# Folding the later batches' sums of squares to a pair of bf16 rows on the VectorE, in a chunk that the scores have left

## The chip, the cores and the metric

The kernel runs on one core of a Trainium2 chip. The metric is the device time of one execution in microseconds (us), over several executions. The profile is one execution with every instruction recorded; its span is 1.9 to 2.0 us shorter than the time. PE is the TensorE (matmuls), PEld its weight loads, DVE the VectorE, ACT the ScalarE, POOL the GpSimd.

## The reference

Attention over channels ("cross-covariance"), then a gated feed-forward layer on all tokens. There are 4 batches of 6016 tokens with 256 channels. Cut to what matters here:

```python
qn = q / (np.linalg.norm(q, axis=1, keepdims=True) + 1e-06)   # norm over the 6016 tokens
kn = k / (np.linalg.norm(k, axis=1, keepdims=True) + 1e-06)
s = kn.transpose(0, 2, 1) @ qn / tau                          # 256 x 256 per batch
a = softmax(s)                                                # per row
x = (v @ a).reshape(B * S, D)
out = (sigmoid(x @ w_gate) * (x @ w_val)) @ w_out
```

## The kernel before

A batch's tokens lie as 47 row tiles of 128 tokens, in 12 chunks (row groups) of up to four tiles; the last has three. While PE runs the feed-forward of batch b, it also works on the scores and norms of batch n = b + 1, spread over "slots". A chunk has 12 slots (FC = 12), and a slot is one gate/value pair with four output matmuls of the chunk before:

```python
for ci in range(NCH):                      # 12 chunks
    block = b + 1 < B and ci in (9, 10)    # these do their output matmuls at the end
    for f in range(FC):                    # 12 slots
        glu(b, ci, f)                      # 4 matmuls of 512 columns, sigmoid on ACT, hT multiply on DVE
        flush()                            # output copies that have become ready, on DVE
        if prev is not None and not block:
            out_mms(*prev, f * TPC, (f + 1) * TPC)   # 4 matmuls of 256 columns
        for fn, a in side.get((ci, f), ()):          # scores, squares, norms of batch n
            fn(*a)
    ...
```

`ps_gate` and `ps_val`, the PSUM buffers that a slot's matmuls write, have two copies each. The value matmul of slot f + 2 must wait until the hT multiply of slot f has read its buffer.

The side work of the next batch: a score is two matmuls of 256 columns per row tile. DVE squares q and k of each group and adds the squares into bf16 accumulators of four rows. The norm step sums these over the partitions with matmuls against ones:

```python
first, last = (14 if b == 0 else 0), 9 * FC
for g, (t0, nt) in enumerate(groups):
    s0 = first + g * (last - first) // NCH
    at(max(0, s0 - 20), load_qk, n, t0, nt)
    for u in range(nt):
        at(first + (t0 + u) * (last - first) // NT, score, n, t0, u)
    ...
    for i, (fn, w) in enumerate(((acc_square, 0), (acc_add, 0), (acc_square, 1), (acc_add, 1))):
        at(s0 + 1 + 2 * i, fn, n, g, w)
at(9 * FC + 9, norms_mm, n)

def norms_mm(b):
    ...
    norm_mms(ps, (acc_q,), TPC, True, True, (0,))     # 4 rows x 2 halves, one column each
    for u in range(TPC):                              # 4 rows, 256 columns each
        mm(ps[:, CB:], ones_bf, acc_k[:, u, :], False, u == TPC - 1, skip_group_check=True)
```

Of the kernel before, what the change touches and what calls it, by code (L numbers as in the profile page):

```python
# [9 lines left out]
FP32 = mybir.dt.float32  # L10
BF16 = mybir.dt.bfloat16
ACT = mybir.ActivationFunctionType
ALU = mybir.AluOpType
# [4 lines left out]
def kernel(  # L18
# [20 lines left out]
    nc = tc.nc  # L39
    P = nc.NUM_PARTITIONS  # L40
# [4 lines left out]
    B, N, C = q.shape  # L45
# [3 lines left out]
    CB = C // P  # L49
    FC = DFF // P  # L50
    FG = 512
    NFG = DFF // FG
    TPC = 4
# [12 lines left out]
    def pool(name, bufs, **kw):  # L66
        return ctx.enter_context(tc.tile_pool(name=name, bufs=bufs, **kw))
# [4 lines left out]
    attp = pool("attp", 1)  # L72
# [14 lines left out]
    def mm(out, lhsT, rhs, start, stop, **kw):  # L87
        nc.tensor.matmul(out, lhsT=lhsT, rhs=rhs, start=start, stop=stop, **kw)  # L88
# [33 lines left out]
    ones_bf = consts.tile([P, P], BF16)  # L122
# [14 lines left out]
    for fg in range(NFG):  # L137
        for w, src in enumerate((moe_w_gate, moe_w_val)):
            nc.gpsimd.dma_start(
                out=w_sb[w][fg],  # L140
                in_=src.rearrange("(t p) f -> p t f", p=P)[:, :, ds(fg * FG, FG)],
# [5 lines left out]
    st = {}  # L147
# [33 lines left out]
    def norm_mms(ps, sqs, nt, first, last, order=(0, 1)):  # L181

        for w in order:
            sq = sqs[w]
            for u in range(nt):
                for j in range(CB):
                    mm(
                        ps[:, w * CB + j : w * CB + j + 1],
                        sq[:, u, ds(j * P, P)],
                        ones_bf[:, 0:1],  # L190
                        start=(first and w == order[0] and u == 0 and j == 0),
                        stop=(last and u == nt - 1),
                        skip_group_check=True,
                    )
# [15 lines left out]
    def acc_add(b, g, w):  # L210
# [5 lines left out]
            out=acc[:, :nt, :], in0=acc[:, :nt, :], in1=st[b]["sq", w][:, :nt, :], op=ALU.add  # L216
        )

    def norms_mm(b):

        s = st[b]
        acc_q, acc_k = s["acc"]
        ps = psm.tile([P, CB + C], FP32, tag="m", name="ps_n")
        norm_mms(ps, (acc_q,), TPC, True, True, (0,))
        for u in range(TPC):
            mm(ps[:, CB:], ones_bf, acc_k[:, u, :], False, u == TPC - 1, skip_group_check=True)
        s["n"] = ps

    def wide_sqrt(b):
# [136 lines left out]
    def transpose_v(b, ci, ps=None, late=None):  # L366

        t0, nt = groups[ci]
        v_sb = vs.pop((b, ci))
        vT = vtpool.tile([P, TPC * CB, P], BF16, tag="vT", name="vT")  # L370
        flat = v_sb[:, :nt, :].rearrange("p t c -> p (t c)")
        if ps is None:
            nc.sync.dma_start_transpose(out=vT[:, : nt * CB, :], in_=flat)
        else:
            for n in range(nt * CB):
                nc.tensor.transpose(  # L376
                    out=ps[:, n, :], in_=flat[:, ds(n * P, P)], identity=ident_bf
                )
            half = nt * CB // 2
            nc.vector.tensor_copy(out=vT[:, :half, :], in_=ps[:, :half, :])  # L380
            (nc.scalar.copy if late is None else late)(vT[:, half : nt * CB, :], ps[:, half : nt * CB, :])
        vts[b, ci] = vT.rearrange("p (u cb) n -> p cb u n", cb=CB)
# [65 lines left out]
    acc = st[0]["acc"]  # L448
# [50 lines left out]
    def side_work(b):  # L499


        side = {}

        def at(slot, fn, *a):
            side.setdefault(divmod(slot, FC), []).append((fn, a))

        for ci in range(NCH):
            nb, nci = (b, ci + 1) if ci + 1 < NCH else (b + 1, 0)
            lb, lci = (b, ci + 2) if ci + 2 < NCH else (b + 1, ci + 2 - NCH)
            if (nb, nci) == (0, 1):  # L510
                at(7, lambda: transpose_v(0, 1, psm.tile([P, TPC * CB, P], BF16, tag="m", name="ps_tp")))
            elif nb < B:
                at(ci * FC + 2, transpose_v, nb, nci)
            if lb < B:
                at(ci * FC + 0, load_v, lb, lci)
        n = b + 1
        if n == B:
            return side
        first, last = (14 if b == 0 else 0), 9 * FC
        for g, (t0, nt) in enumerate(groups):  # L520
            s0 = first + g * (last - first) // NCH
            at(max(0, s0 - 20), load_qk, n, t0, nt)
            for u in range(nt):
                at(first + (t0 + u) * (last - first) // NT, score, n, t0, u)
            if g == 0:
                at(s0, acc_start, n)
            for i, (fn, w) in enumerate(((acc_square, 0), (acc_add, 0), (acc_square, 1), (acc_add, 1))):
                at(s0 + 1 + 2 * i, fn, n, g, w)
        at(9 * FC + 9, norms_mm, n)
        for ci, s, *call in (  # L530
            (9, 0, wide_sqrt, n),
            (9, 2, wide_inv, n, 0),
            (9, 3, wide_inv, n, 1),
            (10, 0, wide_scale, n),
            (10, 0, exps, n, 0),
            (10, 0, exps, n, 1),
        ):
            side.setdefault((ci, FC + s), []).append((call[0], call[1:]))
        at(11 * FC + 0, sums_both, n)
        at(11 * FC + 0, gh_tiles, n)  # L540
        for i in range(len(gh_order)):
            at(11 * FC + min(i + 1, FC - 1), gh, n, i, *((pss, "s"), (psm, "m"))[i % 2])
        return side
# [3 lines left out]
    for b in range(B):  # L547
        side = side_work(b)
        for ci in range(NCH):
            block = b + 1 < B and ci in (9, 10)  # L550
            for f in range(FC):
                glu(b, ci, f)
                flush()
                if prev is not None and not block:
                    out_mms(*prev, f * TPC, (f + 1) * TPC)
                for fn, a in side.get((ci, f), ()):
                    fn(*a)
                if (b, ci) == (0, 0) and f < len(gh_order) - 5:
                    gh(0, 5 + f, pso, "o")
            if prev is not None and block:  # L560
                for s in range(TPC):
                    for fn, a in side.get((ci, FC + s), ()):
                        fn(*a)
                    out_mms(*prev, s * FC, (s + 1) * FC)
                    flush()
            prev = (b, ci)
# [38 lines left out]
```

## Time and profile before

| | before |
|---|---|
| time, median of 6 runs | 831.43 us (831.34 to 831.52) |
| span of the profiled run | 829.6 us |
| PE busy | 817.8 us (99%), 5224 matmuls |
| DVE busy | 581.1 us (70%), 998 instructions |
| norm matmuls of the later batches | 24 of one column, 12 of 256 columns |

PE is the bound. Its matmuls overlap in the record, so the cost of one is read from the start of one to the start of the next. The prediction shows the lines.

### The profile page before, as it was taken

What the parts mean: (1) busy time and instruction counts of PE and PEld (TensorE: products, weight loads), DVE (VectorE), ACT (ScalarE), POOL (GpSimd) and SP (SyncE); (2) the same over time, 40 slices, a digit from 0 to 9 for tenths busy, and PEclk for the clock granted to TensorE, in tenths of its full rate; (3) what the DMA queues carried; (4) which work ended last, traced back from release to release, by engine and by line L of the source; (5) the groups of instructions that cost most, each with busy time, mean ns of one, the idle gap of its engine ahead of it and who ended that gap; (6) DMA issues with size and microseconds to landing.
All of it is one profiled execution on the core that took longest, in us unless ns stands there. A gap on an engine that the chain in (4) does not pass through costs nothing.

```text
span 829.6 us, 13793 instructions
## 1 busy us (share of the span) xinstructions
PE 817.8 (99%) x5224; PEld 503.6 (61%) x5224; DVE 581.1 (70%) x998; ACT 391.9 (47%) x644; POOL 83.3 (10%) x159
## 2 busy tenths in 40 slices
PE   7899999999999999999999999999999999999998
PEld 4556666666666666665576666666566566666666
DVE  6577777777667777777767777777766666666664
ACT  4654444445644444444654444444655444444442
POOL 5531100002110100000210020000000000000000
PEclk9999999999999999999999999999999999999999
DMA  9999724326755553233874453233222323322211
GB/s 209 207 206 185 134 52 90 51 62 131 135 107 102 102 108 62 51 52 84 156 140 100 84 113 73 51 78 63 61 61 64 71 51 83 70 49 69 46 36 71
DMA packets 78739, 77.19 MB, mean 93 GB/s; under 512 B 50768, under 2 KB 55632, under 8 KB 78672
## 3 DMA queue, kind: packets, MB, share of 16 engines
q0 software_dynamic: 23920, 38.81, 28.3%
q1 hardware_dynamic: 54608, 36.97, 17.4%
q8 instruction: 41, 0.67, 0.3%
q10 hardware_dynamic: 144, 0.52, 0.2%
q14 instruction: 26, 0.21, 0.1%
HBM read 78.64 MB, written 24.64 MB: 125 GB/s over the span
## 4 chain that ended last, share of the span: by engine, by line
PE 95%; DMA 3%; POOL 0%; issue 0%; ACT 0%; DVE 0%; POOLq 0%; ACTq 0%
PE ps_o L88 30%; PE ps_val L88 29%; PE ps_gate L88 29%; PE ps_s L88 4%; DMA k_sb<-in_k_dram 3%; PE ps_gh L88 3%; PE ps_n L88 0%; PE ps_busy L88 0%; POOL q_sb L97 0%; ACT e_sb L294 0%; DVE hT L406 0%; ACT g_sb L405 0%; POOL k_sb L97 0%; PE ps_rk L88 0%; PE ps_tp L376 0%
## 5 line engine op out<-in xcount | busy, mean ns | idle before, releaser
L406 DVE TENSOR_TENSOR hT<-ps_val,g_sb 128x512 bf16<-128x512 f32 (+1 forms) x576 | 391.5, 680 | 214.6 <-ACT g_sb L405 209.3
L405 ACT ACTIVATE g_sb<-ps_gate 128x512 bf16<-128x512 f32 (+1 forms) x576 | 338.5, 589 | 386.0 <-PE ps_gate L88 378.4
L88 PE MATMUL ps_gate<-vT,gh_G 128*128 128x512 bf16 (+1 forms) x1152 | 337.7, 375 | 0.4 <-ACT g_sb L405 0.4
L88 PE MATMUL ps_val<-vT,gh_H 128*128 128x512 bf16 (+1 forms) x1152 | 337.5, 375 | 0.1
L88 PE MATMUL ps_o<-w_out_sb,hT 128*128 128x256 bf16 x2256 | 326.2, 273 | 0.0
L88 PEld LDWEIGHTS <-hT 128*128 128x128 bf16 x2256 | 220.8, 98 | 124.7
L88 PEld LDWEIGHTS <-gh_H 128*128 128x128 bf16 x1152 | 112.7, 98 | 131.0 <-issue 0.4
L88 PEld LDWEIGHTS <-gh_G 128*128 128x128 bf16 x1152 | 112.4, 98 | 38.0 <-issue 0.6
L106 POOL DMA_DIRECT2D v_sb<-in_v_dram x48 | 25.6, 534 | 623.6 <-DMA vT<-v_sb 501.3
L432 DVE COPY out_sb<-ps_o 128x256 f32<-128x256 f32 x188 | 77.9, 414 | 13.5 <-PE ps_o L88 13.5
L88 PE MATMUL ps_s<-k_sb,q_sb 128*128 128x256 bf16 x376 | 66.0, 272 | 5.6 <-DMA k_sb<-in_k_dram 4.3
L88 PEld LDWEIGHTS <-q_sb 128*128 128x128 bf16 x376 | 36.6, 98 | 14.7 <-issue 6.8
L215 DVE TENSOR_TENSOR acc<-acc,sq 128x1024 bf16<-128x1024 bf16 (+1 forms) x66 | 44.2, 670 | 0.0
L176 DVE TENSOR_TENSOR sq<-q_sb 128x1024 bf16<-128x1024 bf16 (+2 forms) x44 | 29.4, 668 | 2.7 <-DMA q_sb<-in_q_dram 2.7
L97 POOL DMA_DIRECT2D q_sb<-in_q_dram x48 | 26.4, 550 | 15.3 <-DMA q_sb<-in_q_dram 6.2
L97 POOL DMA_DIRECT2D k_sb<-in_k_dram x48 | 26.2, 545 | 13.9 <-DMA k_sb<-in_k_dram 8.6
L176 DVE TENSOR_TENSOR sq<-k_sb 128x1024 bf16<-128x1024 bf16 (+2 forms) x34 | 22.4, 658 | 0.9 <-ACT sq L174 0.9
L359 ACT ACTIVATE gh_G<-ps_gh,rrow 128x512 bf16<-128x512 f32 x21 | 14.4, 688 | 12.7 <-PE ps_gh L88 10.9
L88 PE MATMUL ps_busy<-ones_wide,ones_bf 128*128 128x512 bf16 x60 | 17.0, 416 | 1.6 <-DVE shift L127 1.6
L174 ACT ACTIVATE sq<-k_sb 128x1024 bf16<-128x1024 bf16 (+1 forms) x11 | 11.2, 1019 | 14.6 <-DMA k_sb<-in_k_dram 14.6
L361 DVE TENSOR_SCALAR gh_H<-ps_gh,rrow 128x512 bf16<-128x512 f32 x22 | 16.4, 744 | 1.6 <-PE ps_gh L88 1.6
L455 DVE TENSOR_TENSOR acc<-acc,sq 128x1024 bf16<-128x1024 bf16 x16 | 11.1, 692 | 5.6 <-ACT sq L174 5.4
(59 smaller groups left out, 117.7 us busy)
## 6 DMA issues: line engine op xcount, KB each, us to landing
out_dram<-out_sb SPq DMA_DIRECT2D x44, 512.0 KB, 2.9
v_sb<-in_v_dram POOLq DMA_DIRECT2D x44, 256.0 KB, 3.9
q_sb<-in_q_dram POOLq DMA_DIRECT2D x43, 256.0 KB, 7.0
k_sb<-in_k_dram POOLq DMA_DIRECT2D x43, 256.0 KB, 7.7
out_dram<-out_sb SPq DMA_DIRECT2D x4, 384.0 KB, 2.5
w_gate<-in_moe_w_gate_dram POOLq DMA_DIRECT2D x3, 256.0 KB, 6.8
w_val<-in_moe_w_val_dram POOLq DMA_DIRECT2D x3, 256.0 KB, 7.4
w_out_sb<-in_moe_w_out_dram POOLq DMA_DIRECT2D x1, 768.0 KB, 12.6
```

Source lines behind the costliest of these rows:

```text
L88: nc.tensor.matmul(out, lhsT=lhsT, rhs=rhs, start=start, stop=stop, **kw)
L97: nc.gpsimd.dma_start(out=tl[:, :nt, :], in_=rows(src, b)[:, t0 : t0 + nt, :])
L106: nc.gpsimd.dma_start(out=v_sb[:, :nt, :], in_=rows(v, b)[:, t0 : t0 + nt, :])
L174: nc.scalar.activation(out=sq[:, :nt, :], in_=src[:, :nt, :], func=ACT.Square)
L176: engine.tensor_tensor(out=sq[:, :nt, :], in0=src[:, :nt, :], in1=src[:, :nt, :], op=ALU.mult)
L215: nc.vector.tensor_tensor(out=acc[:, :nt, :], in0=acc[:, :nt, :], in1=st[b]["sq", w][:, :nt, :], op=ALU.add)
L359: nc.scalar.activation(out=dst, in_=ps, func=ACT.Copy, scale=r)
L361: nc.vector.tensor_scalar(out=dst, in0=ps, scalar1=r, scalar2=None, op0=ALU.mult)
L405: nc.scalar.activation(out=g_sb[:, :n], in_=ps_gate[:, :n], func=ACT.Sigmoid)
L406: nc.vector.tensor_tensor(out=hts[b, ci][:, f, :n], in0=ps_val[:, :n], in1=g_sb[:, :n], op=ALU.mult)
L432: nc.vector.tensor_copy(out=out_sb[:, s, :], in_=ps)
L455: nc.vector.tensor_tensor(out=acc[w], in0=acc[w], in1=sq[w], op=ALU.add)
```

## The change

The intent is to take matmuls off the engine that sets the time. DVE folds the four accumulated rows to one fp32 row, and stores it as two bf16 numbers: the rounded value and what the rounding lost. The norm step then reads two rows in place of four. To make room on DVE, the scores, squares and adds are spread over eight chunks in place of nine, and the folds stand in six slots of the chunk that this frees.

```diff
+    def acc_fold(b, w, step):
+        s = st[b]
+        if step == 0:
+            acc = s["acc"][w]
+            s["two"] = attp.tile([P, 2, C], FP32, tag="two", name="two")
+            nc.vector.tensor_tensor(out=s["two"], in0=acc[:, :2, :], in1=acc[:, 2:, :], op=ALU.add)
+            return
+        one, other = s["two"][:, 0, :], s["two"][:, 1, :]
+        if step == 1:
+            nc.vector.tensor_tensor(out=one, in0=one, in1=other, op=ALU.add)
+            return
+        fold = attp.tile([P, 2, C], BF16, tag=f"fold{w}", name="fold")
+        nc.vector.tensor_copy(out=fold[:, 0, :], in_=one)
+        nc.vector.tensor_tensor(out=fold[:, 1, :], in0=one, in1=fold[:, 0, :], op=ALU.subtract)
+        s.setdefault("fold", []).append(fold)
...
-        norm_mms(ps, (acc_q,), TPC, True, True, (0,))
-        for u in range(TPC):
-            mm(ps[:, CB:], ones_bf, acc_k[:, u, :], False, u == TPC - 1, skip_group_check=True)
+        norm_mms(ps, (fold_q,), 2, True, True, (0,))
+        for u in range(2):
+            mm(ps[:, CB:], ones_bf, fold_k[:, u, :], False, u == 1, skip_group_check=True)
...
-        first, last = (14 if b == 0 else 0), 9 * FC
+        first, last = (14 if b == 0 else 0), 8 * FC
...
+        for i in range(6):
+            at(8 * FC + 2 + i, acc_fold, n, *divmod(i, 3))
```

More of the change, by code (lines that the diff above doesn't have):

```diff
@@ L217, in acc_add @@
         )
+    def acc_fold(b, w, step):
[13 more added lines that the diff above has]
+        s.setdefault("fold", []).append(fold)
     def norms_mm(b):
         s = st[b]
-        acc_q, acc_k = s["acc"]
+        fold_q, fold_k = s["fold"]
         ps = psm.tile([P, CB + C], FP32, tag="m", name="ps_n")
-        norm_mms(ps, (acc_q,), TPC, True, True, (0,))
-        for u in range(TPC):
-            mm(ps[:, CB:], ones_bf, acc_k[:, u, :], False, u == TPC - 1, skip_group_check=True)
+        norm_mms(ps, (fold_q,), 2, True, True, (0,))
+        for u in range(2):
+            mm(ps[:, CB:], ones_bf, fold_k[:, u, :], False, u == 1, skip_group_check=True)
         s["n"] = ps
```

## The prediction

> **What bounds the kernel now.** I read the page first (engine totals, slices, chain), then the waits of the TensorE, then its timeline at the place that the change edits, then the VectorE's groups and timeline. The totals, slices and chain come from the page:
>
> ```profile
> span 829.6 us, 13793 instructions
> ...
> PE 817.8 (99%) x5224; PEld 503.6 (61%) x5224; DVE 581.1 (70%) x998; ACT 391.9 (47%) x644; POOL 83.3 (10%) x159
> ...
> PE   7899999999999999999999999999999999999998
> ...
> PEclk9999999999999999999999999999999999999999
> ...
> PE 95%; DMA 3%; POOL 0%; issue 0%; ACT 0%; DVE 0%; POOLq 0%; ACTq 0%
> ```
>
> The TensorE (PE) is busy for 99% of the span at its full granted clock, and 95% of the chain that ended last is its own work. The 3% of DMA is the opening, where batch 0 loads. A 99% could still hide small waits, so I asked for the waits of PE from 45 us to 800 us; the answer holds one line:
>
> ```profile
> PE ps_gate L88 <- ACT g_sb L405: 0.4, 1, 0.4
> ```
>
> That one lies at 52 us. From 53 us to the end the same view is empty. I also took every interval from one matmul's start to the next in the trace: 216 ns for 512 columns, 109 ns for 256, and after 53 us none is more than 15 ns over its kind. So from 53 us on the time is a plain sum of PE instructions: taking one away must shorten the kernel by that instruction's slot, as long as no other engine makes PE wait.
>
> The place of the change, in the timeline of PE for 196.5 to 199.5 us (start, duration, instruction):
>
> ```profile
> 197.44 0.59 PE L88 MATMUL ps_val<-vT,gh_H 128*128 128x512 bf16 x2
> 197.87 0.34 PE L88 MATMUL ps_n<-ones_bf,acc 128*128 128x1 bf16 x8
> 198.08 0.60 PE L88 MATMUL ps_n<-acc,ones_bf 128*128 128x256 bf16 x4
> 198.51 0.59 PE L88 MATMUL ps_gate<-vT,gh_G 128*128 128x512 bf16 x2
> ```
>
> Read the starts, not the durations, since matmuls overlap: the eight one-column matmuls take 198.08 - 197.87 = 0.21 us (26 ns each), the four of 256 columns 198.51 - 198.08 = 0.43 us (108 ns each). Nothing waits here. The whole norm step is 0.64 us a batch, three times (batches 1 to 3), 1.9 us of 830.
>
> The VectorE (DVE) is the other side of the change. Its groups, shapes kept apart (count, total busy us, mean ns, idle before):
>
> ```profile
> L406 DVE TENSOR_TENSOR hT<-ps_val,g_sb 128x512 bf16<-128x512 f32 x528 | 364.7, 691 | 190.6 <-ACT g_sb L405 187.9 <-PE ps_val L88 0.2
> L432 DVE COPY out_sb<-ps_o 128x256 f32<-128x256 f32 x188 | 77.9, 414 | 13.5 <-PE ps_o L88 13.5
> L215 DVE TENSOR_TENSOR acc<-acc,sq 128x1024 bf16<-128x1024 bf16 x60 | 40.9, 682 | 0.0
> ...
> L129 DVE CAST q_sb<-first 128x1024 bf16<-128x1024 f32 x1 | 0.7, 694 | 4.0 <-DMA first<-in_q_dram 4.0
> ```
>
> The idle time in the first line says that DVE usually waits for the sigmoid on ACT, with 190 us of slack in all.
>
> **What the Trainium skill says.** "VectorE: DVE Perf Modes", section "The TRN2 errata", gives (N+151)/0.96 ns for an fp32 tensor_tensor; for N=512 that is 691 ns, and the trace has 691 for the hT multiply. Its section "The perf-mode tier table" lets bf16 tensor_tensor run at two elements a cycle, fp32 at one, and fp32 tensor_copy at two. The trace agrees: 682 ns for a 1024-wide bf16 add and 694 ns for a 1024-wide cast from fp32, both (512+151)/0.96 = 691 within 1.3%. "TensorE: Matmul & The Clock Gate", section "Back-to-back issue gap", gives N/2.4 + 2.5 ns (109 for 256) and a floor of about 25 ns for a tiny matmul; the trace has 108 and 26. "SBUF — State Buffer", section "SBUF: two separate sides", says that a VectorE operation in a two-port mode locks out GpSimd, which then can't write DMA descriptors; that bears on the new fp32 copies, and no trace of before isolates it.
>
> **The change part by part.**
>
> Removed from PE: per later batch the q norms go from 4 rows x 2 halves = 8 one-column matmuls to 4, the k norms from 4 matmuls of 256 columns to 2. That is 4 x 26 + 2 x 108 = 320 ns a batch, 0.96 us in three. The instruction order of the built kernel confirms 18 matmuls and 18 weight loads fewer (36 rows). All of it is on the path, since PE has no gap there.
>
> Added to DVE: per batch and operand one add of two bf16 row pairs into fp32 (512 wide, not all 16-bit, so one a cycle: 691 ns), one fp32 add (256 wide: (256+151)/0.96 = 424), one cast to bf16 (256 wide at two a cycle: (128+151)/0.96 = 290) and one mixed subtract (424). These are estimates from the formula above, checked against the rows above. The sum is 1.83 us, twice 3.66 a batch, 11.0 us in three batches and 24 instructions. DVE goes from 581 to about 592 us, all beside PE if it fits.
>
> Does it fit? The folds stand in slots 2 to 7 of chunk 8, one slot being one gate/value pair with its share of output matmuls: PE takes 4 x 216 + 4 x 109 = 1.30 us a slot. DVE's real cost is again the spacing of starts. In the timeline of all engines at 175 to 179 us:
>
> ```profile
> 175.11 0.69 DVE L406 TENSOR_TENSOR hT<-ps_val,g_sb 128x512 bf16<-128x512 f32 x1 [0.49 <-ACT g_sb L405]
> ...
> 175.72 0.68 DVE L176 TENSOR_TENSOR sq<-k_sb 128x1024 bf16<-128x1024 bf16 x1
> ...
> 176.41 0.69 DVE L406 TENSOR_TENSOR hT<-ps_val,g_sb 128x512 bf16<-128x512 f32 x1
> ...
> 178.40 0.59 PE L88 MATMUL ps_val<-vT,gh_H 128*128 128x512 bf16 x2
> ```
>
> The hT multiply holds DVE for 0.61 us until the next starts. Over the six slots: 6 x 0.61 (hT) + 2 x 0.34 (output copies, start to start) + 3.66 at full durations, or about 3.0 at spacing = 7.3 to 8.0 us against 6 x 1.30 = 7.8 us of PE. So DVE is about full there and may fall 0.2 us behind. How far may it? The multiply that starts at 176.41 ends at 177.10 and frees the ps_val buffer that the matmul at 178.40 refills: 1.30 us to spare, of which 0.22 us come from a score in between; 1.08 us in a slot without scores. A lag of 0.2 us, even 0.8 with every term at its full length, costs nothing.
>
> Moved: scores, squares and their adds go from 9 chunks to 8, for batch 1 from slots 14 to 107 into slots 14 to 95. The PE work is the same sum in other slots. DVE has 4 operations of 0.68 us per group of rows: with groups every 8 slots, one in every other slot. Two such slots need 2 x 0.61 + 0.61 + 0.34 = 2.2 us against at least 2.6 of PE. In batch 0's run (groups every 6 or 7 slots) two accumulations fall in one slot twice; the worse of them holds hT, an output copy and two accumulations, 0.61 + 0.34 + 1.22 = 2.2 us against 1.3 to 1.5: a lag of at most 0.9 us, under the 1.08. The loads are issued 20 slots ahead and often far earlier: the first for batch 1 at 38 us, its first score at 58 us. Group 1's score moves only one slot (1.3 us) nearer.
>
> Sum: -0.96 us, plus about 0.05 for some small stall: 831.4 - 0.9 = 830.5 us.
>
> **The rivals.** (1) VectorE becomes the bound in the fold slots or in batch 1's squeezed accumulations. For it: DVE is about full there. Against it: the 1.08 us of slack and the short stretch. If each fold operation also paid some 0.1 us of dependency wait, the lag could pass the slack by 0.3 us a batch: some 830.5 + 0.9 = 831.4, no gain. (2) The loads or scores moved forward meet the crowded opening: DMA engines are over 90% busy until about 80 us, and descriptors are written by POOL, which the new copies may block for 0.3 us at a time. For it: PE's waits on k_sb in the opening total 4.3 us. Against it: those are batch 0's; batch 1's loads lead by about 20 us and more, and the later ones by tens of us. If it did happen, it would cost 0.5 to 2 us once. (3) The change frees more than its matmuls, say if the switch of stationary operands costs extra time there; but the spacing of 26 and 108 ns already contains the weight loads, so at most a further 0.1 us a batch, 830.1 us.
>
> **Range and chances.** The executions of before lie within 0.14 us; another chip or another opening may shift everything by some tenths. I put 829.6 to 831.5 as eight in ten: the gain in full with a lucky opening at one end, rival 1 in full at the other. The largest conceivable effect is under 0.3% and the threshold 2%, so within 2% gets 0.985, faster 0.008, slower 0.007.
>
> **What would show it right or wrong.** Right: PE matmuls 5224 to 5206, ps_n of 256 columns from 12 to 6; the norm step 0.32 instead of 0.64 us from start to start; DVE up by 10 to 11 us and 24 instructions, with fold rows near 691, 424, 290 and 424 ns; PE's waits after 53 us still empty; the span near 828.7 us. Wrong: waits of ps_val or ps_gate on DVE hT or ACT g_sb in chunk 8 or in the first 200 us (rival 1), of ps_s on a load (rival 2), or a span that moved by other than about 1 us though PE shows no wait.

## The result, and the profile after

| | before | after |
|---|---|---|
| time, median of 6 runs | 831.43 us | 831.01 us (830.86 to 831.11) |
| span of the profiled run | 829.6 us | 829.0 us |

The median fell by 0.42 us. The ratio is 0.9995 with a 95% interval of 0.9982 to 1.0008, "same" by the 2% rule. A ratio is the mean time of one kernel's fast runs over that of the other's in the same rounds, so not quite the ratio of the medians quoted here. The interval is wider than the effect, so what follows rests on the starts of matmuls in the traces and takes the medians as a second witness.

From the page of the changed kernel:

```profile
span 829.0 us, 13765 instructions
...
PE 816.1 (98%) x5192; PEld 502.6 (61%) x5206; DVE 588.9 (71%) x1022; ACT 391.6 (47%) x644; POOL 83.1 (10%) x159
...
PE 94%; DMA 4%; DVE 1%; issue 0%; POOL 0%; ACT 0%; POOLq 0%; ACTq 0%
```

There are 5206 weight loads, 18 fewer, as the built order had it; the record lacks 14 of the 5206 matmuls, so the matmul count can't be used. DVE ran 24 instructions more. The waits of PE from 45 us on still hold the one line of before, and nothing after 53 us:

```profile
PE ps_gate L88 <- ACT g_sb L422: 0.4, 1, 0.4
```

The norm step in PE's timeline (start, duration):

```profile
197.23 0.59 PE L88 MATMUL ps_val<-vT,gh_H 128*128 128x512 bf16 x2
197.66 0.24 PE L88 MATMUL ps_n<-ones_bf,fold 128*128 128x1 bf16 x4
197.76 0.38 PE L88 MATMUL ps_n<-fold,ones_bf 128*128 128x256 bf16 x2
197.98 0.59 PE L88 MATMUL ps_gate<-vT,gh_G 128*128 128x512 bf16 x2
```

From 197.66 to 197.98 it takes 0.32 us in place of 0.64. So the removal paid: 3 x 0.32 = 0.96 us. The folds, as groups of DVE with shapes kept apart (lines left out between them):

```profile
L225 DVE TENSOR_TENSOR two<-acc 128x512 f32<-128x512 bf16 x6 | 4.1, 682 | 0.0
...
L233 DVE TENSOR_TENSOR fold<-two,fold 128x256 bf16<-128x256 f32 x6 | 2.6, 425 | 0.2
L229 DVE TENSOR_TENSOR two<-two 128x256 f32<-128x256 f32 x6 | 2.5, 416 | 0.0
...
L232 DVE CAST fold<-two 128x256 bf16<-128x256 f32 x6 | 1.7, 283 | 0.0
```

They sum to 10.8 us (six times the four means). The engine's busy time grew by only 7.8 us, since the recorded ends of DVE instructions overlap the next start and are counted once. In the fold slots DVE works without a pause and yet keeps pace. This is its timeline:

```profile
178.59 0.69 DVE L423 TENSOR_TENSOR hT<-ps_val,g_sb 128x512 bf16<-128x512 f32 x1
179.20 0.41 DVE L449 COPY out_sb<-ps_o 128x256 f32<-128x256 f32 x1
179.53 0.41 DVE L229 TENSOR_TENSOR two<-two 128x256 f32<-128x256 f32 x1
179.89 0.69 DVE L423 TENSOR_TENSOR hT<-ps_val,g_sb 128x512 bf16<-128x512 f32 x1
```

One slot of DVE with an output copy and a fold is 179.89 - 178.59 = 1.30 us, which is PE's slot too.

**Where the rest went.** Taking every start-to-start interval of PE after 53 us and comparing it with the usual one for its size (216, 162 or 109 ns) shows three in the changed kernel that are too long: 296 ns too long at 254.7 us, 296 ns at 454.2 us and 71 ns at 608.4 us. (Gaps of 216 ns where one of the 14 unrecorded matmuls belongs are left aside.) The kernel before has none. This is PE's timeline of the changed kernel at the first:

```profile
253.60 0.59 PE L88 MATMUL ps_gate<-vT,gh_G 128*128 128x512 bf16 x2
254.04 0.59 PE L88 MATMUL ps_val<-vT,gh_H 128*128 128x512 bf16 x2
254.47 0.59 PE L88 MATMUL ps_gate<-vT,gh_G 128*128 128x512 bf16 x2
255.20 0.59 PE L88 MATMUL ps_val<-vT,gh_H 128*128 128x512 bf16 x2
255.63 0.38 PE L88 MATMUL ps_o<-w_out_sb,hT 128*128 128x256 bf16 x2
```

The value matmul should start 0.43 us after the gate's, at 254.90, and starts at 255.20. The waits view does not show it, because the modelled end of the gate matmul (254.47 + 0.59) covers much of the wait; only 0.13 us is left as idle time of PE. What it waits for is in DVE's timeline of the same stretch:

```profile
252.92 0.69 DVE L423 TENSOR_TENSOR hT<-ps_val,g_sb 128x512 bf16<-128x512 f32 x1 [0.82 <-ACT g_sb L422]
253.53 0.41 DVE L449 COPY out_sb<-ps_o 128x256 f32<-128x256 f32 x1
253.86 0.68 DVE L176 TENSOR_TENSOR sq<-q_sb 128x1024 bf16<-128x1024 bf16 x1
254.46 1.28 DVE L423 TENSOR_TENSOR hT<-ps_val,g_sb 128x512 bf16<-128x512 f32 x2
```

Number the slots by the code. The last chunk of a batch has three row tiles, so 36 output matmuls, four a slot: they fill slots 0 to 8 of the next batch's first chunk. **Slots 9, 10 and 11 have none**, and a slot there is 4 x 0.216 = 0.86 us of PE, not 1.30. The multiply at 252.92 is that of slot 9. The copy behind it is the last output copy, and the square of row group 1 stands in slot 9. So the multiply of slot 10 starts only at 254.46 and ends 0.68 us later, at 255.14; the value matmul two slots on, in the second chunk's first slot, needs that buffer and starts at 255.20. In the kernel before, the same square stands in slot 10, behind slot 10's multiply. DVE's timeline of before:

```profile
253.23 0.69 DVE L406 TENSOR_TENSOR hT<-ps_val,g_sb 128x512 bf16<-128x512 f32 x1 [0.61 <-ACT g_sb L405]
253.84 0.41 DVE L432 COPY out_sb<-ps_o 128x256 f32<-128x256 f32 x1
254.31 0.69 DVE L406 TENSOR_TENSOR hT<-ps_val,g_sb 128x512 bf16<-128x512 f32 x1
254.92 0.68 DVE L176 TENSOR_TENSOR sq<-q_sb 128x1024 bf16<-128x1024 bf16 x1
```

Here slot 10's multiply starts 1.08 us after slot 9's; in the changed kernel, 1.54 us.

To leave the opening out, take the steady stretch: from the start of the first output matmul (55.041 us before, 54.830 after) to the start of the last matmul. It is 770.525 us before and 770.223 us after, 0.302 us less. The account is -0.96 + 2 x 0.296 + 0.071 = -0.30. The opening was 0.21 us shorter in this profile. Over the nine profiles it ends between 54.83 and 55.05 us, and PE's work in it is the same in all.

### The profile page after: what moved, and what is told of

Its sections match the earlier page's. It is cut to its first block, busy times and chain, and to the rows that moved or that the text cites. A ratio compares the mean times of both kernels' runs of the same rounds, so it can differ in the third digit from the quotient of the medians.

```text
span 829.0 us, 13765 instructions
## 1 busy us (share of the span) xinstructions
PE 816.1 (98%) x5192; PEld 502.6 (61%) x5206; DVE 588.9 (71%) x1022; ACT 391.6 (47%) x644; POOL 83.1 (10%) x159
## 4 chain that ended last, share of the span: by engine, by line
PE 94%; DMA 4%; DVE 1%; issue 0%; POOL 0%; ACT 0%; POOLq 0%; ACTq 0%
PE ps_o L88 30%; PE ps_gate L88 29%; PE ps_val L88 29%; PE ps_s L88 4%; DMA q_sb<-in_q_dram 3%; PE ps_gh L88 2%; DMA w_val<-in_moe_w_val_dram 1%; DVE hT L423 0%; ACT g_sb L422 0%; DVE sq L176 0%; PE ps_n L88 0%; POOL k_sb L97 0%; POOL q_sb L97 0%; PE ps_tp L393 0%; DVE out_sb L449 0%
```

## The experiments

**Theory:** removed matmuls are worth their slots in full; the new pace, not the folds, gives back 0.6 us through two waits in the short slots. **Rivals:** the matmuls were never worth more than what was gained; the folds took it; the denser accumulations in general took it. In the table, each kernel stands against the kernel before of the same rounds (medians 831.37 and 831.44 us), and the steady stretch against 770.525 us. "Stall" is an interval of PE after 53 us over its kind, one profile each.

| kernel | median us | minus before | stretch minus before | stalls, ns |
|---|---|---|---|---|
| changed | 831.01 | -0.42 | -0.302 | 296, 296, 71 |
| halved_norms | 830.44 | -0.93 | -0.957 | none |
| pace_only | 832.00 | +0.63 | +0.586 | 297, 295 |
| group1_early | 831.62 | +0.25 | +0.149 | 79, 78 |
| repaired | 830.55 | -0.82 | -0.887 | 71 |
| score_moved | 830.65 | -0.79 | -0.732 | 79, 78, 72 |
| folds_unused | 831.43 | -0.01 | +0.069 | 70 |
| one_row | 830.03 | -1.41 | -1.367 | 71 |

The 95% intervals of the ratios are about 0.13% (1.1 us) wide to each side. Only one_row's excludes 1 (0.9970 to 0.9995). Four single runs came out 1.25 to 1.7 us over the median of their kind, at a granted clock of 0.997 or 0.998 in place of 0.999 to 1.0; they pull the means, not the medians. They are not what makes the intervals wide: that of the changed kernel, which has no such run on either side, is as wide. What carries the argument is that in each of the eight kernels the stretch is the slots taken away plus the listed stalls, to within 0.01 us. The medians lie within 0.12 us of the stretch.

### The matmuls alone: halved_norms

```diff
-        norm_mms(ps, (acc_q,), TPC, True, True, (0,))
-        for u in range(TPC):
-            mm(ps[:, CB:], ones_bf, acc_k[:, u, :], False, u == TPC - 1, skip_group_check=True)
+        norm_mms(ps, (acc_q,), 2, True, True, (0,))
+        for u in range(2):
+            mm(ps[:, CB:], ones_bf, acc_k[:, u, :], False, u == 1, skip_group_check=True)
```

> The kernel before, with the norm matmuls of the later batches on two of the four accumulated rows and nothing else changed (no folds, scores over nine chunks; the result is wrong on purpose). My theory (removed matmuls are worth their slots in full, and the change gave some back in new VectorE waits): 0.96 us under the kernel before, about 830.5 us, and no new interval on the TensorE over its kind after 53 us. Rival (the removed matmuls were never worth more than what the change gained, because something hides them): about 0.4 us under the kernel before.

830.44 us, 0.93 us under the kernel before, and 0.957 us in the steady stretch. The matmuls are worth their slots. The norms are wrong here, yet the comparison with the reference passed: the likely reason, which no run measured, is that the scores are so small that the softmax hardly moves. So that comparison can't judge how exact the norms of any variant are.

### The pace alone: pace_only

```diff
-        first, last = (14 if b == 0 else 0), 9 * FC
+        first, last = (14 if b == 0 else 0), 8 * FC
```

> The kernel before with only the pace changed: the next batch's scores, squares and adds over eight chunks in place of nine; norms on four rows, no folds. My theory: two stalls of 0.30 us on the TensorE at the first slot of the second chunk of batches 1 and 2, as in the changed kernel, so 0.6 us over the kernel before, about 832.0 us. Rival (the folds took back the gain): within 0.1 us of the kernel before.

832.00 us, 0.63 us over the kernel before, with the two stalls and no other. PE's timeline of this kernel:

```profile
254.37 0.59 PE L88 MATMUL ps_val<-vT,gh_H 128*128 128x512 bf16 x2
254.80 0.59 PE L88 MATMUL ps_gate<-vT,gh_G 128*128 128x512 bf16 x2
255.53 0.59 PE L88 MATMUL ps_val<-vT,gh_H 128*128 128x512 bf16 x2
```

Again 0.73 us from gate to value in place of 0.43. There is no fold in this kernel, so the folds do not make the stalls.

### One accumulation in the kernel before: group1_early

```diff
-                at(s0 + 1 + 2 * i, fn, n, g, w)
+                at(s0 + 1 + 2 * i - (1 if b > 0 and g == 1 else 0), fn, n, g, w)
```

> The kernel before with one thing moved: in the first chunk of batches 1 and 2 the square and the add of row group 1 stand one slot earlier (slots 9, 11, 13, 15 in place of 10, 12, 14, 16); scores stay over nine chunks. My theory (slots 9 to 11 of that chunk hold no output matmuls, so a slot is short there and a square in slot 9 behind an output copy makes the VectorE free a ps_val buffer late): both stalls of about 0.30 us appear, about 832.0 us. Rival (the stalls come from the higher density of all groups): no stall, within 0.1 us of the kernel before.

This was half a miss. The stalls came, at the same two places, but with 79 and 78 ns in place of 300: the density of the other groups is not needed for a stall, and yet the square's slot is not all of it. The difference, 296 - 79 = 217 ns, is just one score (two matmuls of 256 columns). In this kernel the scores stand in slots 9 and 11, so two lie between slot 9's value matmul and the one that waits; in the changed kernel they stand in slots 8 and 10, and only one does. The new pace took a score out of the stretch that DVE had to catch up in.

### The accumulation moved back in the changed kernel: repaired

```diff
-                at(s0 + 1 + 2 * i, fn, n, g, w)
+                at(s0 + 1 + 2 * i + (1 if b > 0 and g == 1 else 0), fn, n, g, w)
```

> The changed kernel with only row group 1's square and add moved back one slot in batches 1 and 2 (10, 12, 14, 16 in place of 9, 11, 13, 15). My theory: both stalls gone and the whole 0.96 us kept: about 830.4 us, 0.6 us under the changed kernel. Rival (the folds or the pace of the rest took the gain): the same as the changed kernel, about 831.0 us.

830.55 us, both stalls gone. In PE's timeline of this kernel the value matmul follows the gate's by 0.43 us:

```profile
254.60 0.59 PE L88 MATMUL ps_gate<-vT,gh_G 128*128 128x512 bf16 x2
255.03 0.59 PE L88 MATMUL ps_val<-vT,gh_H 128*128 128x512 bf16 x2
```

The steady stretch is 0.887 us under before: 0.96 less the 0.071 that stays. Moving one row group by one slot won back 0.59 us of the stretch against the changed kernel (0.40 us by the medians, each against the kernel before of its own rounds).

### One score moved in the changed kernel: score_moved

```diff
-                at(first + (t0 + u) * (last - first) // NT, score, n, t0, u)
+                at(first + (t0 + u) * (last - first) // NT + (1 if b > 0 and t0 + u == 4 else 0), score, n, t0, u)
```

> The changed kernel with its accumulations as they are (row group 1 at slots 9, 11, 13, 15), but in batches 1 and 2 the score of row 4 goes from slot 8 to slot 9 of the first chunk, so that two scores in place of one lie between the ps_val matmul of slot 9 and that of the next chunk's first slot. My theory (each score of 0.217 us there lengthens the time that the VectorE has): the two stalls shrink from 0.296 to 0.079 us each, so about 0.43 us under the changed kernel, 830.6 us. Rival (only the slot of the square counts, not the scores): both stalls stay at 0.30 us and the time at 831.0 us.

The stalls shrank to 79 and 78 ns, the predicted size, with the square still in slot 9. So the stall has two terms: DVE's extra instruction, and the PE work between slot 9's value matmul, whose multiply opens DVE's run without a pause, and the value matmul that waits.

### The folds as pure extra work: folds_unused

```diff
# the repaired kernel, with
-        fold_q, fold_k = s["fold"]
-        norm_mms(ps, (fold_q,), 2, True, True, (0,))
-        for u in range(2):
-            mm(ps[:, CB:], ones_bf, fold_k[:, u, :], False, u == 1, skip_group_check=True)
+        acc_q, acc_k = s["acc"]
+        norm_mms(ps, (acc_q,), TPC, True, True, (0,))
+        for u in range(TPC):
+            mm(ps[:, CB:], ones_bf, acc_k[:, u, :], False, u == TPC - 1, skip_group_check=True)
```

> The repaired kernel (group 1 moved back one slot), folds computed as in the change, but the norms still taken from the four accumulated rows, so the folds are pure extra work on the VectorE and nothing is removed from the TensorE. My theory (the folds cost nothing): within 0.1 us of the kernel before, 831.4 to 831.5 us, no stall in the fold slots. Rival (the folds slow something by themselves): over the kernel before by 0.3 us or more.

831.43 us, 0.01 us from the kernel before, and no stall in the fold slots. One of 70 ns stands at 608.9 us, far from any fold (the last is at 584 us). All five kernels with folds have it, at 608 to 613 us, and none of the four without. There one hT multiply follows 0.40 us of idle time of DVE in place of the 0.17 of its neighbours, though its sigmoid is done. It costs 0.07 us.

The traces narrow down what holds it. In all five kernels the held multiply is number 1216 in DVE's recorded order; in one_row, with 12 fold instructions fewer, that number comes 5 us later, and the stall with it. A multiply before which DVE stood idle usually starts 0.03 us after its sigmoid ends. In the nine traces, after 54 us, 27 of them start 0.26 to 0.28 us after it, and all 27 stand at numbers that lie a multiple of 128 apart (448, 576, 704, 960, 1216, 1344, 1472 or 1600); four at number 832 are not late. PE lost time in five of the 27. This points to the place in DVE's instruction order: 24 more instructions moved such a place into a short slot. In the five stalls a transfer of 8 KB of instructions starts 0.67 to 0.69 us after the start of the held multiply; whether the loading of instructions is the cause was not tested.

### One row in place of two: one_row

```diff
# the repaired kernel, with
         if step == 1:
-            nc.vector.tensor_tensor(out=one, in0=one, in1=other, op=ALU.add)
-            return
-        fold = attp.tile([P, 2, C], BF16, tag=f"fold{w}", name="fold")
-        nc.vector.tensor_copy(out=fold[:, 0, :], in_=one)
-        nc.vector.tensor_tensor(out=fold[:, 1, :], in0=one, in1=fold[:, 0, :], op=ALU.subtract)
-        s.setdefault("fold", []).append(fold)
+            fold = attp.tile([P, 1, C], BF16, tag=f"fold{w}", name="fold")
+            nc.vector.tensor_tensor(out=fold[:, 0, :], in0=one, in1=other, op=ALU.add)
+            s.setdefault("fold", []).append(fold)
...
# and norms_mm on that one row
```

> The repaired kernel with the fold to a single bf16 row, without the second number that holds the rounding error: the norm step then has 2 one-column matmuls and 1 of 256 columns a batch in place of 8 and 4, and two of the four fold instructions per operand go. My theory (time is the sum of the matmuls' slots): 3 x (6 x 26 + 3 x 108) ns = 1.44 us under the kernel before, about 830.0 us, about 0.5 us under the repaired kernel. Rival (what is left at the norm step can't shrink further, because the weight loads of 98 ns show): no gain over the repaired kernel, 830.5 us.

830.03 us, the fastest, 1.41 us under the kernel before. PE's timeline of its norm step:

```profile
197.88 0.19 PE L88 MATMUL ps_n<-ones_bf,fold 128*128 128x1 bf16 x2
197.93 0.27 PE L88 MATMUL ps_n<-fold,ones_bf 128*128 128x256 bf16 x1
198.04 0.59 PE L88 MATMUL ps_gate<-vT,gh_G 128*128 128x512 bf16 x2
```

The step is 198.04 - 197.88 = 0.16 us. The price is one more rounding to bf16 of a number that was summed in bf16 anyway. That this is harmless is argued, not shown, since the comparison passed even with half of the rows left out.

## Why the prediction was right or wrong

**The time.** 830.5 was predicted and 831.01 measured, inside the range, and "within 2%" was right. Of the gain, 0.9 us predicted, 0.42 came. The upper end of the range had been drawn for rival 1 in the fold slots; that it also covered stalls elsewhere is luck.

**The bound and the removal: right.** PE is a plain sum from 53 us on, and the norm step went from 0.64 to 0.32 us. halved_norms shows the 0.96 us alone.

**The folds: right.** 682, 416, 283 and 425 ns against 691, 424, 290 and 424, and 10.8 us in sum against 11.0. DVE was full in those slots and did not hold PE up; folds_unused shows that they are free but for the 0.07 us.

**The step that failed** is "about 0.05 for some small stall", and behind it the sentence "Two such slots need 2 x 0.61 + 0.61 + 0.34 = 2.2 us against at least 2.6 of PE". It took 1.30 us for every slot. In slots 9 to 11 of the first chunk of batches 1 and 2 a slot is 0.86 us, as the last chunk of a batch has only 36 output matmuls to give. There the moved square met the last output copy, and one score left the stretch: two stalls of 0.296 us in place of 0.05 in all. (The third stall, 0.071 us, is near the 0.05 by chance: the prediction gave no reason for one there.) pace_only shows that the pace makes them, repaired and score_moved what they are made of.

**The rivals.** Rival 1 had the right mechanism (DVE frees ps_val late and the matmul waits) and the wrong places: it looked at the fold slots and at batch 1's squeezed accumulations, and neither stalled. It named 0.9 us, and 0.59 was true. Rival 2 (loads or scores in the crowded opening) did not happen: no score waits for a load after 45 us, and POOL's load instructions took the same on average (q_sb 545 ns in place of 550, k_sb 549 in place of 545). Rival 3 (more gained than the matmuls) is excluded by halved_norms.

**The signs.** "PE's waits after 53 us still empty" was called a sign of being right, and it was empty although 0.66 us were lost. The sign was badly chosen; start-to-start intervals would have been the one. "DVE up by 10 to 11 us" missed, at 7.8, for the overlap told above. One sign of being wrong did come: the span moved by 0.6 us in place of about 1 though the waits view of PE stayed empty.

## What to carry to other kernels

Here one engine was the bound and its work a plain sum, and the matmuls taken away were worth their start-to-start slots (0.957 us measured, 0.96 counted); a small change of schedule elsewhere gave 0.59 us of that back. Before moving side work between slots, list the slots that are shorter than the rest (ends of ragged chunks), and add up there what the engine that frees a double buffer has to do, from where it last stood idle, against the time until the buffer is needed again. Look for lost time in start-to-start intervals, not in the idle time of an engine whose ends are modelled.

## What the Trainium skill lacked or had wrong

- "TensorE: Matmul & The Clock Gate", section "Back-to-back issue gap", gives 131 ns a matmul for a sustained stream of weight loads and matmuls at N=512, and calls N/2.4 + 2.5 ns the isolated gap. Here streams with a weight load for each matmul run at 216 ns for N=512 and 109 ns for N=256, which is what the isolated formula gives.
- No page gives the size of a wait that a matmul's modelled end can hide (it would belong to "Perfetto Trace Analysis"): in the changed kernel two waits of 0.30 us each left 0.13 us of idle time of PE, and no line in the waits view.
- No page gives a delay at fixed places of VectorE's instruction order (it would belong to "Advanced Engine Details and Errata"): here 27 multiplies, at places that lie a multiple of 128 instructions apart, started 0.26 to 0.28 us after their sigmoid in place of 0.03, and four at such a place did not.
